# Second layer of a two-layer MLP: Strassen products over pairs of 512-token blocks instead of over the halves of one block

## The chip, the cores and the metric

One core of one Trainium2 chip. The metric is the device time of one execution in microseconds (us), the median of several runs.

## What is computed

An attention with few packed keys gives x (4608 tokens of 512 features). Two feed-forward layers follow, each 512 to 2048 to 512 features:

```python
def _moe_ref(x, w_in, w_out):
    h = x @ w_in                                   # 4608x512 @ 512x2048
    sp = np.where(h > 20.0, h, np.log1p(np.exp(np.minimum(h, 20.0))))
    g = h * np.tanh(sp)
    return (g @ w_out).astype(np.float32)          # 4608x2048 @ 2048x512

def _moe2_ref(x, w_in, w_out):
    h = x @ w_in
    g = h - np.tanh(h)
    return (g @ w_out).astype(np.float32)

attn_out = _attn_ref(**attn_kwargs)                # 8 batches, 8 heads, 576 tokens, 64 features
x = np.ascontiguousarray(attn_out.transpose(0, 2, 1, 3)).reshape(B * S, H * D)
x = _moe_ref(x=x, **moe_kwargs)
return _moe2_ref(x=x, **moe2_kwargs)
```

All of it is float32. Each matrix product is made of three passes over operands split into a high and a low part (high by high, high by low, low by high; `PASSES`), each a matmul of its own.

## The kernel before

**Blocks.** Tokens lie along the columns. There are nine blocks of 512 tokens: blocks 0 to 7 are the first 512 tokens of each batch, block 8 (the rest block) is the last 64 of all eight. The first layer (`layer1`, `layer1_rest`) leaves its output y of each block in DRAM (`y_d`).

**Second layer.** For each block, `load_y` loads y, and ScalarE (ACT) and VectorE (DVE) make from it the seven Strassen operands, split into high and low. Strassen's two by two runs over two halves of the features, two halves of w_in's 2048 columns, and two halves of the block's tokens, `HB` = 256 columns each. The seven combinations of the weights were made earlier and lie in `w2i_d`. `pair2` does one pair p of 128-wide chunks (fc = p and p + 8) of the 2048: seven products of six matmuls of 256 columns each (L856), the copies of three of them out of PSUM by ACT (L867), the additions into h by DVE (L870), and the last copy by ACT (L888). `second` then computes g of each chunk with 5 ACT and 6 DVE instructions, and adds g times w_out into four accumulators, `acc`, with 12 matmuls of 512 columns (L923). So a pair is 42 matmuls of 256 columns and 24 of 512. After eight pairs the accumulators are copied out (L929) and stored. All of w_out (16 tiles `wo` of 512 KB) is loaded once (`load_second`) and stays; each pair's weights `m` come anew for each block.

**Order.** A planner (`Plan.emit`) writes the instructions of all engines out in one order: every operation has a key (a due time), costs and buffers, and each engine takes the available operation of the lowest key. On the chip each engine follows its own list in order, waiting on semaphores. All loads and stores are issued by SyncE (SP), in its list's order, through the helper at L323. Buffers are taken from named kinds (`wo`, `a2`, `x`, `m`, `bk` for PSUM banks), some of them in the order of the keys (`queue`).

Of the kernel before, what the change touches and what calls it, by code (L numbers as in the profile page):

```python
# [49 lines left out]
class Buf:  # L50
# [21 lines left out]
class Plan:  # L72
# [44 lines left out]
    def emit(self):  # L117
# [18 lines left out]
        while left:  # L136
# [107 lines left out]
def tile_packed_attention_mish_tanhshrink(  # L244
# [43 lines left out]
    for nm, n in (("yh", 7), ("tt", 2), ("pc", 6)):  # L288
# [9 lines left out]
    w2o_d = dr.tile([16, 128, 2, 512], F32, name="w2o_d")  # L298

# [492 lines left out]
    def load_y(blk, sw):  # L792
        k0 = kb(NPAIR * blk) - 8
        f, ld = [], []
        for i in range(2):
            f.append(Buf(K["yv" if i == 0 else "yh"], [128, 2, TB]))
            ld.append(dma(lambda i=i: f[i].tile,
                          lambda i=i: y_d[2 * i:2 * i + 2, :, blk * TB:(blk + 1) * TB].rearrange("k p t -> p k t"), 512,
                          k0 - 15 + i, [y_st[blk, i], sw], [f[i]]))
# [12 lines left out]
        def split(j, kd, i, t, after, k):  # L812
# [5 lines left out]
            yq[blk, j], yq_rd[blk, j] = o, l  # L818
# [5 lines left out]
        st1 = split(2, "yh", 0, 0, [t1], k0 + 2.6)  # L824
        t3 = sub(0, 1, (1, 1), (0, 1), [t1] + ld, k0 + 3.3)
        s22 = split(4, "yh", 1, 1, ld[1:], k0 + 3.9)
        t2 = sub(1, 1, (1, 1), (0, 0), [s22, t1, t3], k0 + 4.6)
        st2 = split(3, "yh", 1, 1, [t2], k0 + 5.2)
        t4 = sub(1, 0, (1, 1), (1, 0), [t2, s21], k0 + 6.0)
        split(5, "yh", 0, 1, [t3], k0 + 6.5)  # L830
        split(6, "yh", 1, 0, [t4], k0 + 7.8)

    acc2, o_, g4_last = {}, {}, {}

    def pair2(n, sw):
# [12 lines left out]
        def product(j, slot, bk, deps, take, first):
            w = (wm[j // 4], wm_rd[j // 4])
# [13 lines left out]
        hb = [Buf(K["x"], [128, TB]) for _ in range(2)]
        c1, c5, cy = (Buf(K["pc"], [128, HB]) for _ in range(3))

        def copy(c, bk, slot, deps):
            return op("ACT", a_cost(HB, True), lambda: A.activation(c.tile, bk.tile[:, :HB], AF.Copy), ks(slot), deps, [c])  # L867

        def add(half, tok, bk, c, slot, deps, take, give):
            return op("DVE", v_cost(HB), lambda: V.tensor_tensor(  # L870
                out=hb[half].tile[:, HB * tok:HB * tok + HB], in0=bk.tile[:, :HB], in1=c.tile, op=ALU.add),
                ks(slot), deps, take, give)
# [13 lines left out]
        c22 = add(1, 1, ba, c5, 21, [p7, s5], [hb[1]], [c5])
        p4 = product(6, 30, ba, [p7, c22], [], False)
        c21 = op("ACT", a_cost(HB, True), lambda: A.activation(hb[1].tile[:, :HB], ba.tile[:, :HB], AF.Copy),  # L888
                 ks(31), [p4, c22], give=[ba])
        second(blk, p, hb[0], [c11, c12], ks(20), k0, (41, 42, 43, 44))  # L890
        second(blk, p + 8, hb[1], [c21, c22], ks(32), k0, (52, 53, 54, 55))
# [139 lines left out]
```

## Time and profile before

| | |
|---|---|
| Median of 3 runs | 1484.35 us (1483.98 to 1485.32) |
| The profiled execution | 1483.46 us, of which the span of the profile is 1481.7 us |
| Granted TensorE clock, mean | 0.999 |
| TensorE (PE) busy | 1463.3 us, 99% of the span |
| VectorE (DVE) busy | 1032.4 us, 70% |
| ScalarE (ACT) busy | 993.2 us, 67% |
| DMA moved | 298.52 MB, 201 GB/s |

An engine's busy time is the time in which it has an instruction running, so PE is without work for some 18 us of the span. The stages follow each other on the same engines: attention and first layer up to about 715 us, second layer from there.

### The profile page before, as it was taken

Reading aid. Unit: us, or ns where it says so; the run is one execution under the profiler, and the core shown is the slowest. Engines: PE = TensorE matmul, PEld = TensorE weight load, DVE = VectorE, ACT = ScalarE, POOL = GpSimd, SP = SyncE. Lnnn points to the kernel's source line nnn. Section 1 sums busy time; section 2 is a strip of 40 time slices with the busy share of each in tenths; the row PEclk is TensorE's granted clock in tenths of the full one; section 3 lists DMA queues with packets and bytes.
Section 4 is the critical chain, followed back from the end, with each engine's and each line's share of the span. In section 5 each row is a group of like instructions: output and inputs, shape, how many; then the busy total and the mean of one; then the engine's idle time right before and its main releaser. Section 6 shows DMA issues by size and latency. Waiting matters only on the chain.

```text
span 1481.7 us, 26083 instructions
## 1 busy us (share of the span) xinstructions
PE 1463.3 (99%) x10078; PEld 1273.0 (86%) x10078; DVE 1032.4 (70%) x1924; ACT 993.2 (67%) x1980; POOL 0.2 (0%) x4
## 2 busy tenths in 40 slices
PE   8999999999999999999999999999999999999998
PEld 5898888788888888888898989999999999999996
DVE  6995575746575524214589797888979797888885
ACT  5987675766666555434577667676867676776765
POOL 0000000000000000000000000000000000000000
PEclk9999999999999999999999999999999999999999
DMA  9897585857674532238655546464646565555552
GB/s 335 266 328 257 178 277 185 262 177 253 211 254 161 172 113 76 82 127 299 233 197 207 199 181 227 180 226 153 253 153 224 182 224 184 203 203 193 190 187 51
DMA packets 118380, 298.52 MB, mean 201 GB/s; under 512 B 31856, under 2 KB 41200, under 8 KB 109040
## 3 DMA queue, kind: packets, MB, share of 16 engines
q1 hardware_dynamic: 117968, 296.66, 57.9%
q8 instruction: 79, 1.29, 0.4%
q14 instruction: 45, 0.37, 0.1%
q10 hardware_dynamic: 288, 0.20, 0.0%
HBM read 246.48 MB, written 50.33 MB: 200 GB/s over the span
## 4 chain that ended last, share of the span: by engine, by line
PE 94%; DMA 3%; ACT 2%; DVE 0%; issue 0%; SPq 0%; ACTq 0%
PE acc L923 26%; PE acc L699 26%; PE bk L856 24%; PE bk L729 13%; PE bk L667 2%; PE bk L585 1%; DMA m<-w2i_d 1%; PE bk L537 1%; PE bk L611 0%; PE bk L564 0%; DMA y_d<-yv 0%; DMA st<-in_w1o 0%; DMA st<-in_w1i 0%; DMA x<-in_q 0%; DMA ident<-in_eye 0%; ACT st L343 0%
## 5 line engine op out<-in xcount | busy, mean ns | idle before, releaser
L699 PE MATMUL acc<-g,wo 128*128 128x512 f32 (+2 forms) x1920 | 430.6, 372 | 1.1 <-DVE wo L365 0.7
L923 PE MATMUL acc<-g,wo 128*128 128x512 f32 x1728 | 407.6, 390 | 1.2 <-ACT g L912 1.0
L699 PEld LDWEIGHTS acc<-g,wo 128*128 128x128 f32 x1920 | 327.9, 188 | 64.6 <-issue 11.9
L923 PEld LDWEIGHTS acc<-g,wo 128*128 128x128 f32 x1728 | 318.8, 188 | 65.4 <-ACT g L912 1.4
L856 PE MATMUL bk<-yh,m 128*128 128x256 f32 x2160 | 297.4, 283 | 1.2 <-DMA m<-w2i_d 0.5
L856 PEld LDWEIGHTS bk<-yh,m 128*128 128x128 f32 x2160 | 280.7, 191 | 9.4 <-DVE x L870 2.3
L729 PEld LDWEIGHTS bk<-a,m 128*128 128x128 f32 x1536 | 216.5, 188 | 19.4 <-issue 3.5
L729 PE MATMUL bk<-a,m 128*128 128x288 f32 x1536 | 229.2, 296 | 1.5 <-DVE m L678 0.8
L719 DVE TENSOR_TENSOR g<-e,g 128x512 fp32r<-128x512 f32 (+2 forms) x144 | 99.1, 689 | 147.6 <-ACT g L718 146.1
L733 ACT ACTIVATE e<-bk 128x288 f32<-128x288 f32 x256 | 103.6, 409 | 141.8 <-PE bk L729 140.5
L912 ACT ACTIVATE g<-xw 128x512 fp32r<-128x512 f32 x144 | 90.6, 629 | 150.2 <-DVE xw L910 145.7
L870 DVE TENSOR_TENSOR x<-bk,pc 128x256 f32<-128x256 f32 x216 | 89.7, 418 | 83.4 <-PE bk L856 83.4
L856 PE MATMUL bk<-a,m 128*128 128x256 f32 x864 | 127.2, 283 | 0.0
L913 DVE TENSOR_TENSOR g<-xw,g 128x512 fp32r<-128x512 f32 x144 | 99.2, 689 | 37.3 <-ACT g L912 37.2
L856 PEld LDWEIGHTS bk<-a,m 128*128 128x128 f32 x864 | 114.1, 192 | 0.4 <-ACT x L888 0.2
L910 DVE COPY_PREDICATED xw<-e,tt 128x512 f32<-128x512 uint32 x144 | 109.2, 759 | 1.7
L902 DVE SCALAR_TENSOR_TENSOR xw<-xw,xw 128x512 f32<-128x512 f32 x144 | 98.6, 685 | 8.0 <-ACT xw L900 7.9
L718 ACT ACTIVATE g<-e 128x512 fp32r<-128x512 f32 (+2 forms) x144 | 91.0, 632 | 19.1 <-PE acc L699 15.2
L898 ACT ACTIVATE xw<-e,c_qb 128x512 f32<-128x512 f32 x144 | 102.8, 714 | 0.0
L908 DVE TENSOR_TENSOR tt<-x,tt 128x512 f32<-128x512 f32 x144 | 98.9, 687 | 1.4 <-ACT tt L901 0.9
L897 ACT ACTIVATE e<-x 128x512 f32<-128x512 f32 x144 | 90.6, 629 | 13.6 <-DVE x L870 11.6
L906 DVE SCALAR_TENSOR_TENSOR xw<-xw,x 128x512 f32<-128x512 f32 x144 | 98.8, 686 | 0.0
(107 smaller groups left out, 1255.4 us busy)
## 6 DMA issues: line engine op xcount, KB each, us to landing
m<-w2i_d SPq DMA_DIRECT2D x72, 1024.0 KB, 5.1
m<-w2i_d SPq DMA_DIRECT2D x72, 768.0 KB, 6.2
xw<-w1i_d SPq DMA_DIRECT2D x112, 256.0 KB, 4.1
w2i_d<-x SPq DMA_DIRECT2D x56, 256.0 KB, 2.8
x<-in_q SPq DMA_DIRECT2D x64, 144.0 KB, 3.8
y_d<-yv SPq DMA_DIRECT2D x18, 512.0 KB, 4.3
out_t<-x SPq DMA_DIRECT2D x36, 256.0 KB, 2.7
st<-in_w1i SPq DMA_DIRECT2D x16, 512.0 KB, 5.2
```

Of the source, the lines that this page charges most:

```text
L699: T.matmul(ac.tile[:, c0:c1], r(wo[fc].tile[:, wl, oc * 128:(oc + 1) * 128]), r(gv(gl)), start=first and c0 == 0 and i == 0, stop=last and ...
L719: return gt, op("DVE", v_cost(n), lambda: V.tensor_tensor(out=r(gt.tile[:, 1]), in0=ev(), in1=gt.tile[:, 0], op=ALU.subtract), kf + 1.2, [ ...
L729: T.matmul(h.tile[:, :HALF], r(m.tile[:, fc % 4, kc, wl, :]), r(x.tile[:, kc, al, :]), start=(i == 0), stop=(i == 5))
L733: return op("ACT", a_cost(HALF, True), lambda: A.activation(out(), h.tile[:, :HALF], AF.Mish), k0 - 2.5, [g1] + after, take, [h], table="m ...
L856: T.matmul(bk.tile[:, :HB], r(wv[:, kc, wl, :]), r(yq[blk, j].tile[:, kc, yl, :]), start=(first and i == 0), stop=(i == 5), skip_group_che ...
L898: p1 = op("ACT", a_cost(TB, False, True), lambda: A.activation(s1.tile, zz.tile, AF.Sigmoid, bias=c_qb, scale=Q_L), k0 + 0.1, [sq], [s1])
L902: q = op("DVE", v_cost(TB), lambda: V.scalar_tensor_tensor(out=s1.tile, in0=s1.tile, scalar=Q_E, in1=s2.tile, op0=ALU.add, op1=ALU.mult), ...
L906: q = op("DVE", v_cost(TB), lambda: V.scalar_tensor_tensor(out=s1.tile, in0=s1.tile, scalar=Q_A, in1=h.tile, op0=ALU.mult, op1=ALU.mult), ...
L908: d = op("DVE", v_cost(TB), lambda: V.tensor_tensor(out=tt.tile, in0=h.tile, in1=tt.tile, op=ALU.subtract), k0 + 1.3, [th], give=[h])
L910: q = op("DVE", v_cost(TB), lambda: V.copy_predicated(s1.tile, zz.tile.bitcast(U32), tt.tile), k0 + 1.4, [q, d, k], give=[zz, tt])
L913: lo = op("DVE", v_cost(TB), lambda: V.tensor_tensor(out=r(gt.tile[:, 1, :]), in0=s1.tile, in1=gt.tile[:, 0, :], op=ALU.subtract), k0 + 2. ...
L923: T.matmul(ac.tile, r(w2c[fc].tile[:, wl, oc * 128:(oc + 1) * 128]), r(gt.tile[:, gl, :]), start=(fc == 0 and i == 0), stop=(fc == NFC - 1 ...
```

## The change

The blocks 0 to 7 are taken in pairs (super-blocks 0 to 3), and Strassen's two token halves are now the two blocks of a pair: a product has 512 columns. The rest block stays as it was, with 256. Four things go with it:

- The operands of the four super-blocks are made while the first layer runs (`combos`), written to DRAM (`yq_d`), and loaded by `load_sup`: 14 loads of 512 KB for a super-block, into four `a2` and ten `wo` buffers.
- These take the place of w_out, which is now fetched anew for each block (`fetch_out`), with at most six tiles held at a time (`cap_w`).
- `products` and the output matmuls have keys of their own (`prod_key`, `out_key`): a pair's products give h of both blocks; the first block's outputs run between the products, the second block's later, among the next super-block's first products. h of the second block waits in 13 buffers `hq`.
- A planner rule for queued buffers is loosened (`b in k.queue[:need[k]]`), and the Sigmoid and Tanh table is loaded earlier.

```diff
-                                    turn = turn and (k.queue is None or k.queue[0] is b)
+                                    turn = turn and (k.queue is None or b in k.queue[:need[k]])
...
+    yq_d = dr.tile([B // 2, 7, 2, 128, 2, TB], F32, name="yq_d")
...
+    C0, C1 = (103, 109, 115, 128.5), 14.0
+
+    def combos(s, kc):
+
+        k0 = ka(C0[s]) + C1 * kc
+        late = s == NSUP - 1
...
+        def split(j, i, t, after, k):
+            o, ov = bufs("xw", j)
+            h = op("ACT", a_cost(TB), lambda: A.activation(r(ov(0)), b(i, t), AF.Copy), k, after, o)
+            l = op("DVE", v_cost(TB), lambda: V.tensor_tensor(
+                out=r(ov(1)), in0=b(i, t), in1=ov(0), op=ALU.subtract), k + 0.5, [h], give=held((i, t)))
...
-    def load_second(sw):
-        for fc in range(NFC):
-            w2c[fc] = Buf(K["wo"], [128, 2, 512])
-            w2c_rd[fc] = dma(lambda fc=fc: w2c[fc].tile, lambda fc=fc: w2o_d[fc], 512,
-                             kb(fc % 8) + fc // 8, [w2_st[16 + fc], sw], [w2c[fc]])
...
+    PR, OU = 9.52, 5.44
+    PER = NPAIR * (PR + 2 * OU)
+
+    def base(s):
+        return ka(NA + NFC) - NPAIR * OU + s * PER
+
+    def prod_key(s, p):
+        if s == NSUP:
+            return base(s) + 23 + (PR + OU) * p
+        return base(s) + (22 + 20 * p if p < 2 else 62.6 + (PR + OU) * (p - 2))
...
+    def fetch_out(s, half, p):
+        for c in range(2):
+            fc = p + 8 * c
+            w = w2c[s, half, fc] = Buf(K["wo"], [128, 2, 512], cap=K["cap_w"])
+            w2c_rd[s, half, fc] = dma(lambda w=w: w.tile, lambda fc=fc: w2o_d[fc], 512,
+                                      out_key(s, half, p) - 12 + c, [w2_st[16 + fc]], [w])
...
+    def load_sup(s):
+        for n, j in enumerate(range(7)):
+            for kc in range(2):
+                yq[s, j, kc] = Buf(K["a2" if j < 2 else "wo"], [128, 2, TB])
+                yq_rd[s, j, kc] = dma(lambda j=j, kc=kc: yq[s, j, kc].tile, lambda j=j, kc=kc: yq_d[s, j, kc], 512,
+                                      prod_key(s, 0) - 24 + 1.5 * n, yq_st[s, j, kc], [yq[s, j, kc]])
...
-                        T.matmul(bk.tile[:, :HB], r(wv[:, kc, wl, :]), r(yq[blk, j].tile[:, kc, yl, :]),
-                                 start=(first and i == 0), stop=(i == 5),
+                        y = ys[kc].tile[:, yl, :] if full else ys[0].tile[:, kc, yl, :]
+                        T.matmul(bk.tile[:, :n], r(wv[:, kc, wl, :]), r(y), start=(first and i == 0), stop=(i == 5),
                                  skip_group_check=not first)
...
-        p1 = product(0, 2, ba, [act2[0]], [ba], True)
-        s1 = copy(c1, ba, 3, [p1])
-        p2 = product(1, 4, bb, [], [bb], True)
-        c11 = add(0, 0, bb, c1, 5, [p2, s1], [hb[0]], [bb, c1])
-        p5 = product(2, 6, bc, [], [bc], True)
-        s5 = copy(c5, bc, 7, [p5])
-        p6 = product(3, 16, ba, [p1, s1], [], False)
+        p1 = product(0, 0, ba, [sw], [ba], True)
+        s1 = copy(c1, ba, 0.5, [p1])
+        p2 = product(1, 1, bb, [], [bb], True)
+        c11 = add(0, 0, bb, c1, 1.5, [p2, s1], [bb, c1])
+        p5 = product(2, 2, bc, [], [bc], True)
+        s5 = copy(c5, bc, 2.5, [p5])
+        p6 = product(3, 3, ba, [p1, s1], [], False)
+        sy = copy(cy, ba, 3.5, [p6])
+        p3 = product(4, 4, bc, [p5, s5], [], False)
+        c12 = add(0, 1, bc, cy, 4.5, [p3, sy, c11], [bc, cy])
+        p7 = product(5, 5, ba, [p6, sy], [], False)
+        c22 = add(1, 1, ba, c5, 5.5, [p7, s5], [c5])
+        p4 = product(6, 6, ba, [p7, c22], [], False)
```

**Where the order changes: a pair's products on PE.** Before, in the middle of the second layer, the seven products (lines L856, a row of six matmuls each) of neighbouring pairs stand interleaved (m_9632 and m_9621 are the weights of two pairs), and each is followed by another bank's product:

```order
L856 MATMUL bk_9625<-yh_8819,m_9632 128x256 x6
L856 MATMUL bk_9746<-yh_9756,m_9621 128x256 x6
L856 MATMUL bk_9877<-a_2_8874,m_9741 128x256 x6
L856 MATMUL bk_9790<-yh_9694,m_9754 128x256 x6
L856 MATMUL bk_9900<-a_3_8893,m_9741 128x256 x6
L856 MATMUL bk_9746<-yh_9777,m_9754 128x256 x6
L856 MATMUL bk_9922<-yh_8979,m_9741 128x256 x6
L923 MATMUL acc_0_9107<-g_9840,wo_7934 128x512 x3
```

Now, within super-block 0, one pair's products (L942 of the changed kernel, two rows of three matmuls each; here the third to the seventh) stand in one run on three banks, two output groups (L1027) ahead of the last:

```order
L942 MATMUL bk_10422<-wo_9230,m_10175 128x512 x3
L942 MATMUL bk_10422<-wo_9235,m_10175 128x512 x3
L942 MATMUL bk_10391<-wo_9247,m_10175 128x512 x3
L942 MATMUL bk_10391<-wo_9252,m_10175 128x512 x3
L942 MATMUL bk_10422<-wo_9267,m_10220 128x512 x3
L942 MATMUL bk_10422<-wo_9273,m_10220 128x512 x3
L942 MATMUL bk_10391<-wo_9279,m_10220 128x512 x3
L942 MATMUL bk_10391<-wo_9283,m_10220 128x512 x3
L1027 MATMUL acc_0_10044<-g_10271,wo_10090 128x512 x3
L1027 MATMUL acc_0_10050<-g_10271,wo_10090 128x512 x3
L942 MATMUL bk_10391<-wo_9303,m_10220 128x512 x3
L942 MATMUL bk_10391<-wo_9306,m_10220 128x512 x3
```

The fifth product writes bank bk_10422 again, one product after the third left it, and the sixth bk_10391 one product after the fourth; the last follows the sixth on one bank with six output matmuls between.

**Where the order changes: SP's loads at the turn of a block.** Before, at the turn from one block to the next, SP's list holds the pairs' weights and two loads of y:

```order
L323 DMA m_9741<-w2i_d 128x2048
L323 DMA m_9754<-w2i_d 128x1536
L323 DMA yv_9798<-y_d 128x2x512
L323 DMA yh_9823<-y_d 128x2x512
L323 DMA m_9872<-w2i_d 128x2048
L323 DMA m_9884<-w2i_d 128x1536
```

Now, at the turn from super-block 0 to 1, the 14 operand loads stand together (the first eight, four into `a_`, four into `wo_`, are ahead of these rows), with both weights of the second pair among them, and the next tiles of w_out come behind:

```order
L324 DMA m_10780<-w2i_d 128x2048
L324 DMA wo_10791<-yq_d 128x1024
L324 DMA wo_10797<-yq_d 128x1024
L324 DMA wo_10803<-yq_d 128x1024
L324 DMA wo_10807<-yq_d 128x1024
L324 DMA wo_10827<-yq_d 128x1024
L324 DMA wo_10830<-yq_d 128x1024
L324 DMA m_10838<-w2i_d 128x1536
L324 DMA wo_10845<-w2o_d 128x1024
L324 DMA wo_10873<-w2o_d 128x1024
L324 DMA wo_10902<-w2o_d 128x1024
L324 DMA wo_10930<-w2o_d 128x1024
```

On PE, 138 matmuls of 512 columns stand from the first product of super-block 0's last pair to the first that reads wo_10845: that pair's 42, 24 and 48 of outputs, and the first 24 of super-block 1's products.

**Where the order changes: PE's end.** Before, 36 matmuls stand behind the last product:

```order
L856 MATMUL bk_16477<-yh_15684,m_16473 128x256 x6
L923 MATMUL acc_0_15963<-g_16645,wo_7934 128x512 x3
L923 MATMUL acc_0_15973<-g_16645,wo_7934 128x512 x3
L923 MATMUL acc_0_15980<-g_16645,wo_7934 128x512 x3
L923 MATMUL acc_0_15985<-g_16645,wo_7934 128x512 x3
L923 MATMUL acc_0_15963<-g_16673,wo_7948 128x512 x3
```

Now it is 69 (the rest of one chunk, of which these rows show the start, and five whole ones of 12):

```order
L942 MATMUL bk_15125<-wo_14156,m_14967 128x256 x6
L1027 MATMUL acc_0_14628<-g_15001,wo_14867 128x512 x3
L1027 MATMUL acc_0_14637<-g_15001,wo_14867 128x512 x3
L1027 MATMUL acc_0_14644<-g_15001,wo_14867 128x512 x3
L1027 MATMUL acc_0_14618<-g_15037,wo_14894 128x512 x3
L1027 MATMUL acc_0_14628<-g_15037,wo_14894 128x512 x3
```

The last product moved ahead of 33 more output matmuls.

## Rows read from the trace of the kernel before

**Rows 1.** The page, part 1: busy time, share, instructions.

```profile
PE 1463.3 (99%) x10078; PEld 1273.0 (86%) x10078; DVE 1032.4 (70%) x1924; ACT 993.2 (67%) x1980; POOL 0.2 (0%) x4
```

**Rows 2.** Windows: length, busy time by engine (PE, PEld, DVE, ACT, POOL), clock, DMA.

```profile
909.00:1246.00 337.00, 336.86 (x2109) 304.94 (x2109) 282.95 (x524) 241.17 (x492) 0.00 (x0) 1.00 0.55 200
580.00:660.00 80.00, 80.00 (x488) 68.08 (x487) 24.05 (x37) 35.34 (x69) 0.00 (x0) 1.00 0.30 97
660.00:707.00 47.00, 47.00 (x222) 39.47 (x222) 18.56 (x29) 19.29 (x32) 0.00 (x0) 1.00 0.77 271
707.00:740.00 33.00, 32.02 (x198) 28.55 (x197) 20.32 (x40) 20.20 (x42) 0.00 (x0) 1.00 0.70 246
1451.00:1482.00 31.00, 23.41 (x116) 19.07 (x114) 17.61 (x32) 14.76 (x28) 0.00 (x0) 0.94 0.16 35
```

**Rows 3.** The chain that ended last, 815 to 990 us: start, length, work.

```profile
818.76 5.49 PE acc L923 x24
...
834.75 5.03 PE bk L856 x42
839.78 5.47 PE acc L923 x24
...
903.16 5.47 PE acc L923 x24
```

**Rows 4.** Groups of instructions: the second layer's matmuls.

```profile
L923 PE MATMUL acc<-g,wo 128*128 128x512 f32 x1728 | 407.6, 390 | 1.2 <-ACT g L912 1.0 <-DVE g L913 0.2
...
L856 PE MATMUL bk<-yh,m 128*128 128x256 f32 x2160 | 297.4, 283 | 1.2 <-DMA m<-w2i_d 0.5 <-DVE x L870 0.4
...
L856 PE MATMUL bk<-a,m 128*128 128x256 f32 x864 | 127.2, 283 | 0.0
```

**Rows 5.** Groups: reads of PSUM by ACT and DVE, of 256 and 512 columns.

```profile
L870 DVE TENSOR_TENSOR x<-bk,pc 128x256 f32<-128x256 f32 x216 | 89.7, 418 | 83.4 <-PE bk L856 83.4
...
L867 ACT ACTIVATE pc<-bk 128x256 f32<-128x256 f32 x216 | 79.3, 370 | 5.6 <-PE bk L856 5.6
...
L678 DVE TENSOR_TENSOR m<-bk,m 128x512 fp32r<-128x512 f32 x64 | 42.1, 676 | 6.6 <-ACT m L676 6.6
...
L929 ACT ACTIVATE x<-acc 128x512 f32<-128x512 f32 x36 | 19.7, 605 | 1.8 <-PE acc L923 1.6
```

**Rows 6.** Waits of PE's weight loads, 740 to 1414 us: total, times, longest.

```profile
PEld bk L856 <- DVE x L870: 1.6, 7, 0.2
```

**Rows 7.** Timeline of ACT, 840 to 862 us: start, length, instruction, idle before.

```profile
846.00 0.38 ACT L888 ACTIVATE x<-bk 128x256 f32<-128x256 f32 x1 [0.20 <-PE bk L856]
...
850.17 0.72 ACT L898 ACTIVATE xw<-e,c_qb 128x512 f32<-128x512 f32 x1
850.79 0.62 ACT L900 ACTIVATE xw<-e 128x512 f32<-128x512 f32 x1
```

**Rows 8.** Groups: one of y's operand instructions on DVE.

```profile
L815 DVE TENSOR_TENSOR yh<-yh,yh 128x512 fp32r<-128x512 f32 x27 | 18.5, 686 | 2.1 <-ACT yh L814 2.1
```

**Rows 9.** DMA issues: count, size, median us to landing.

```profile
m<-w2i_d SPq DMA_DIRECT2D x72, 1024.0 KB, 5.1
m<-w2i_d SPq DMA_DIRECT2D x72, 768.0 KB, 6.2
...
wo<-w2o_d SPq DMA_DIRECT2D x16, 512.0 KB, 4.4
```

**Rows 10.** Windows of 5 us with much DMA; columns as in rows 2.

```profile
680.00:685.00 5.00, 5.00 (x24) 4.14 (x23) 1.39 (x2) 1.26 (x2) 0.00 (x0) 1.00 0.98 343
685.00:690.00 5.00, 5.00 (x24) 4.14 (x23) 2.96 (x5) 2.77 (x5) 0.00 (x0) 1.00 1.05 419
```

**Rows 11.** Timeline of the end, 1464 to 1475 us.

```profile
1464.79 0.88 PE L856 MATMUL bk<-yh,m 128*128 128x256 f32 x6
...
1472.15 0.49 PE L923 MATMUL acc<-g,wo 128*128 128x512 f32 x1 [1.01 <-ACT g L912]
...
1472.87 2.79 PE L923 MATMUL acc<-g,wo 128*128 128x512 f32 x11 [0.23 <-DVE g L913]
```

More of the change, by code (lines that the diff above doesn't have):

```diff
@@ L845, in pair2, with product @@
             wm_rd.append(dma(lambda i=i: wm[i].tile, lambda j0=j0, j1=j1: w2i_d[p, :, j0:j1], 256 * (j1 - j0),
-                             k0 - 26 + 11 * i, [w2_st[p, j] for j in range(j0, j1)] + [sw], [wm[i]]))
-        def product(j, slot, bk, deps, take, first):
-            w = (wm[j // 4], wm_rd[j // 4])
+                             k0 - 20 + 5 * i, [w2_st[p, j] for j in range(j0, j1)], [wm[i]]))
+        def product(j, i, bk, deps, take, first):
+            ys = [yq[s, j, kc] for kc in range(2 if full else 1)]
             def f():
@@ L862, in pair2 @@
         ba, bb, bc = (bank(K["cap_2"]) for _ in range(3))
[L863 to L872, printed above, removed]
@@ L886, in pair2, with hv @@
[L886 to L891, printed above, removed]
-    def second(blk, fc, h, rd, k0, k1, slots):
-        zz, tt, s1 = Buf(K["e"], [128, TB]), Buf(K["tt"], [128, TB]), Buf(K["xw"], [128, TB])
-        s2 = Buf(K["xw"], [128, TB])
+        if full:
+            hb = [[Buf(K["x"], [128, TB]), Buf(K["hq" if p < 6 else "x"], [128, TB])] for _ in range(2)]
+            def hv(half, tok):
+                return hb[half][tok].tile
+        else:
+            hb = [[Buf(K["x"], [128, TB])] * 2 for _ in range(2)]
+            def hv(half, tok):
+                return hb[half][0].tile[:, HB * tok:HB * tok + HB]
@@ new lines, in products, with copy, add @@
+        c1, c5, cy = (Buf(K["pc"], [128, TB]) for _ in range(3))
+        def copy(c, bk, i, deps):
+            return op("ACT", a_cost(n, True), lambda: A.activation(c.tile[:, :n], bk.tile[:, :n], AF.Copy), ks(i) - 12, deps,
+                      [c])
+        def add(half, tok, bk, c, i, deps, give):
+            take = [hb[half][tok]] if full or half == tok else []
+            return op("DVE", v_cost(n), lambda: V.tensor_tensor(
+                out=hv(half, tok), in0=bk.tile[:, :n], in1=c.tile[:, :n], op=ALU.add), ks(i) - 12, deps, take, give)
@@ new lines, in products @@
+        c22 = add(1, 1, ba, c5, 5.5, [p7, s5], [c5])
+        p4 = product(6, 6, ba, [p7, c22], [], False)
+        c21 = op("ACT", a_cost(n, True), lambda: A.activation(hv(1, 0), ba.tile[:, :n], AF.Copy),
+                 ks(6.5) - 12, [p4, c22], [hb[1][0]] if full else [], give=[ba])
+        ev = ((c11, c12), (c21, c22))
+        for half in range(2):
+            fc = p + 8 * half
+            if not full:
+                second(s, 0, fc, hb[half][0], list(ev[half]), ks(7 + 2 * half), out_key(s, 0, p) + OU / 2 * half)
+                continue
+            second(s, 0, fc, hb[half][0], [ev[half][0]], ks(4 + 3 * half), out_key(s, 0, p) + OU / 2 * half)
+            second(s, 1, fc, hb[half][1], [ev[half][1]], ks(25 + 5 * half), out_key(s, 1, p) + OU / 2 * half)
@@ L896, in second @@
+    def second(s, half, fc, h, rd, k0, ko):
+        zz, tt, s1, s2 = (Buf(K[k], [128, TB]) for k in ("e", "tt", "xw", "xw"))
         gt = Buf(K["g"], [128, 2, TB])
+        first, last = fc == 0, fc == NFC - 1
         sq = op("ACT", a_cost(TB), lambda: A.activation(zz.tile, h.tile, AF.Square), k0, rd, [zz])
         p1 = op("ACT", a_cost(TB, False, True), lambda: A.activation(
-            s1.tile, zz.tile, AF.Sigmoid, bias=c_qb, scale=Q_L), k0 + 0.1, [sq], [s1])
-        p2 = op("ACT", a_cost(TB), lambda: A.activation(s2.tile, zz.tile, AF.Tanh, scale=Q_T), k0 + 0.15, [sq], [s2])
@@ L913, in second @@
         lo = op("DVE", v_cost(TB), lambda: V.tensor_tensor(
[L914 removed]
+            out=r(gt.tile[:, 1, :]), in0=h.tile, in1=gt.tile[:, 0, :], op=ALU.subtract), max(k0 + 2.1, ko - 5.9), [a],
+            give=[h])
+        w = w2c[s, half, fc]
         for oc in range(4):
[L916 to L919 removed]
+            if first:
+                acc2[s, half, oc] = Buf(K["acc", oc], [128, 512])
+            ac = acc2[s, half, oc]
@@ L921, in f @@
             def f(oc=oc, ac=ac):
                 for i, (wl, gl) in enumerate(PASSES):
-                    T.matmul(ac.tile, r(w2c[fc].tile[:, wl, oc * 128:(oc + 1) * 128]), r(gt.tile[:, gl, :]),
-                             start=(fc == 0 and i == 0), stop=(fc == NFC - 1 and i == 2))
-            g4_last[oc] = z = op("PE", 0.69, f, ko, [lo, w2c_rd[fc], g4_last.get(oc)],
-                                 [ac] if fc == 0 else [], [gt])
-            if fc == NFC - 1:
+                    T.matmul(ac.tile, r(w.tile[:, wl, oc * 128:(oc + 1) * 128]), r(gt.tile[:, gl, :]),
+                             start=(first and i == 0), stop=(last and i == 2))
```

166 lines of the change are left out of this document (112 added, 54 removed).

## The prediction, made before the changed kernel was run

> **What bounds it now.** I read the page's busy times first: PE is busy 99% of the span, DVE 70%, ACT 67% [rows 1]. The windows by stage say where the rest is: in the middle of the second layer PE is busy 336.86 of 337 us, in the late first layer all of 80 and of 47; only the stretch between the layers (0.98 us idle of 33) and the end (7.6 of 31) leave PE without work [rows 2]. So the time is the sum of PE's matmuls, and other engines, queues and transfers count only where they make PE wait. The chain shows the beat of the second layer: 42 matmuls of 256 columns in 5.03 us, then 24 of 512 in 5.47 us, over and over [rows 3]. That is 119.8 ns for a matmul of 256 columns and 227.9 ns for one of 512: half the columns cost 53% of the time, so each matmul carries a fixed part of about 11.7 ns (2 x 119.8 - 227.9). The means in the groups (283 and 390 ns) are lengths of overlapping records and no price [rows 4].
>
> **The change, part by part.** The sum is made against the profiled execution, 1483.46 us (span 1481.7 and 1.8 around it), which lies 0.9 us under the median of 1484.35; the difference is then put on the median.
>
> *Products.* Of 3024 matmuls of 256 columns [rows 4] the order of the changed kernel keeps 336 (the rest block's 8 pairs of 42). 2688 go, 1344 of 512 columns come. For one pair of chunks and two blocks: 2 x 5.03 = 10.06 us before; 42 x 0.2279 = 9.57 now; 0.49 us less, 32 times: **-15.6 us**. The output matmuls stay as they are. No row has a product of 512 columns; the nearest row is the output matmul, which has the same shapes, a weight load for each matmul, and accumulates in PSUM, so I take its price. The bounds are that price and two narrow ones (no gain).
>
> *Block turns.* Eight pairs take 8 x 10.50 = 84.0 us, but from one block's turn to the next it is 903.16 - 818.76 = 84.40 [rows 3]. In the second layer PE's weight loads wait 7 times, 0.2 us each, for the DVE addition L870 [rows 6], about once a block. At the turn y's operands are made on DVE (11 instructions of 0.69 us for a block [rows 8]), and the addition stands behind one. The change moves this work into the first layer, so I take the eight turns' 0.40 as gone: **-3.2 us** (bounds 0 and -3.2).
>
> *End.* Before, behind the last product, which ends at about 1465.7, PE runs 24 matmuls and then stands 1.01 and 0.23 us for the last g [rows 11]. The g that waited longest was there 7.2 us after that product (1472.87). Now 69 matmuls, 15.7 us, stand behind the last product, so g is there in time: **-1.2 us** (bounds 0 and -1.2).
>
> *Copies out of PSUM.* New in the order is a tight place: a bank is written again one product, 1.37 us, after it was left, twice behind an ACT copy, once behind a DVE addition. ACT begins 0.20 us after PE's end [rows 7] and takes 0.61 for 512 columns [rows 5]: 0.81, so 0.56 is left, and an instruction under way holds ACT for at most 0.62 (850.17 to 850.79 [rows 7]): late by 0.06 at worst. DVE takes 0.68 [rows 5], 0.88 with the start, 0.49 left; an instruction of 0.69 [rows 8] under way makes it late by 0.20 at worst, which is what the longest wait of before was [rows 6]. At worst 32 x (0.06 + 0.06 + 0.20) = 10 us; the worst needs an instruction that has just begun each time, so I take 0.05 a pair: **+1.5 us** (bounds 0 and 10). What hides the copies is the next product alone; without that cover it would be 0.8 us for each.
>
> *Load of the engines.* DVE was busy 282.95 of 337 us, 84% [rows 2]. It loses y's 11 x 0.69 = 7.6 us of each 84.4 (9%), and for two blocks three additions of 0.68 take the place of six of 0.418 [rows 5], 2% more: some 73%. ACT loses as well. Neither becomes the bound.
>
> *Turns of super-blocks.* w_out is now streamed, and the 14 operand loads can start only as the last pair frees their buffers; behind them in SP's list stand the next tiles of w_out, for which PE waits. From the end of that pair's first product to the first matmul that reads such a tile PE has the 138 matmuls counted in the order less that product: 138 x 0.2279 - 1.37 = 30.1 us. In that time 14 x 512 + 1024 + 768 + 512 KB = 9.70 MB must pass. At the 343 to 419 GB/s of busy windows [rows 10] this is 28.3 to 23.1 us; the last tile then needs what a lone load takes beyond its bytes, 4.4 [rows 9] - 1.3 = 3.1 us. So it lands between 3.9 us early and 1.3 late. I take **+0.5 us** for the three such turns (bounds 0 and 4). Elsewhere in a super-block the volume is far from the limit: some 41 MB in 164 us, 250 GB/s, where it was 200 [rows 2]. The Trainium skill (DMA: Bandwidth & Descriptors, section Bandwidth) speaks against this: it puts the HBM limit of one core at about 358 GB/s. By it the 9.70 MB take 27.1 us and the tile lands 0.1 late, which leaves the sum where it is; the window of 419 GB/s shows that for 5 us more can pass.
>
> *From first to second layer.* Here the most is added: between the first operand load and the last store of super-block 3's operands, SP's list now holds 14 operand loads, 28 stores of 256 KB, 8 loads of y, the rest block's loads, six weights and first tiles of w_out, about 30.6 MB in some 95 us of PE's matmuls: 322 GB/s, where 271 and 246 were moved [rows 2]. Stores that wait for ACT and DVE stand ahead of operand loads in the one queue, and six products of the first pair each wait for such a load. Queueing made the 768 KB load land later than the 1024 KB one, 6.2 to 5.1 us [rows 9]; if each of the six is late by that 1.1 us, it is 6.6 us. Most have output matmuls of the rest block ahead of them, so I take a third: **+2 us** (bounds 0 and 6.6).
>
> *First layer.* The other six half-combinations add 42 ACT copies (26 us at 0.61), 66 DVE instructions (45 us at 0.69), and 28 MB within some 140 us. ACT was busy 35.34 of 80 us there, DVE 24.05, DMA moved 97 GB/s, PE was never idle [rows 2]: all of it has room. What could cost is an ACT or DVE instruction that waits for its load with Mish evacuations behind it: **+0.5 us** (bounds 0 and 3).
>
> Sum: -15.6 - 3.2 - 1.2 + 1.5 + 0.5 + 2 + 0.5 = **-15.5 us**: 1468.0 for such a profiled execution, 1468.9, so **1469** us, for the median.
>
> **Rivals.** *Transfers eat half of it.* If the turns get only 320 GB/s, a tile lands 30.3 + 3.1 - 30.1 = 3.3 us late, three times 10 us, or the transition takes its 6.6 and the copies half their bound: 1475 to 1481. For it: 9.70 MB follow each other without a pause, and a window at 0.98 of the engines' time moved only 343 GB/s. Against it: 419 in the next. At 302 GB/s the gain would be gone.
>
> *The DVE addition becomes the bound: slower.* If one more DVE instruction than the one under way stands ahead of the addition before the last product, the product waits 0.20 + 0.68 + 2 x 0.69 - 1.37 = 0.89 us in each of 32 pairs, 28.5 us in the place of the 1.5: about 1496. It decides from about 0.5 us a pair on. For it: before, neighbouring pairs were interleaved and gave every bank more cover. Against it: DVE has a quarter of its time free, and its list has a single instruction between this addition and the one before it.
>
> *The wide product costs two narrow ones.* Then the -15.6 is missing: about 1484. For it: no product of that width is in the trace. Against it: 1728 output matmuls of that width run at 227.9 ns in the same stream [rows 3, 4]. The Trainium skill (TensorE: Matmul & The Clock Gate, section Back-to-back issue gap) gives a matmul N/2.4 + 2.5 ns, 109 and 216 ns; by that the saving is 1344 x 2.5 ns = 3.4 us and the time about 1481. The rows show a fixed part more than four times as large, and they decide.
>
> *All costs are nothing:* -20.0 us, about 1464.
>
> **Chances.** Forecast (1465 to 1475) 0.64; costs nothing or a dearer fixed part (under 1465) 0.08; transfers (1475 to 1481) 0.18; wide product no cheaper 0.04; slower by the addition 0.06. The range 1462 to 1478 holds the first two and half of the third, 0.8. A measurement tells some 0.2% (3 us) from no change: faster 0.90, same 0.04, slower 0.06.
>
> **What would show it.** The chain of the changed kernel in mid super-block: 24 wide products in 5.47 us, six more at 1.37 each, no idle time on PE in that stretch beyond tenths of a us a pair; waits of PE for ACT copies and DVE additions under 3 us in all; no wait for w_out tiles or operands of over 1 us at the three turns; no wait over 0.3 us behind the last product; between the layers PE idle of about 3 us. The prediction is wrong if a product of six takes 1.44 us, if PE waits for the DVE addition in each pair by more than 0.3 us, or if the DMA windows at the turns stay under 320 GB/s.

## The result and the profile after

The changed kernel takes **1462.99 us** (median of six runs, 1460.96 to 1469.62); the kernel before takes 1485.39 beside it (six runs, 1483.98 to 1490.25). The ratio is 0.9854, 95% interval 0.9829 to 0.9879: faster by 22.4 us, 1.5%, where 15.5 us were forecast. The profiled execution takes 1462.25 us with a span of 1460.1, against 1483.46 and 1481.7: 21.6 us of span to account for.

The page's busy times, as in [rows 1]:

```profile
PE 1444.2 (99%) x8734; PEld 1201.1 (82%) x8734; DVE 1026.1 (70%) x1828; ACT 981.8 (67%) x1852; POOL 0.2 (0%) x4
```

PE still bounds the kernel: 19.1 us of the 21.6 are busy time of PE, the other 2.5 its idle time (18.4 before, 15.9 now).

The windows by stage, with the columns of [rows 2]: the late first layer, the stretch between the layers, the second layer, the end.

```profile
660.00:707.00 47.00, 46.57 (x211) 38.49 (x210) 20.16 (x31) 21.51 (x36) 0.00 (x0) 1.00 0.93 343
707.00:740.00 33.00, 33.00 (x148) 27.31 (x147) 22.51 (x38) 20.77 (x38) 0.00 (x0) 1.00 0.94 345
740.00:1414.00 674.00, 674.00 (x3071) 558.75 (x3070) 534.07 (x921) 460.35 (x847) 0.00 (x0) 1.00 0.70 248
1420.00:1461.00 41.00, 34.14 (x189) 29.30 (x188) 20.92 (x38) 18.56 (x35) 0.00 (x0) 0.97 0.28 87
```

In 674 us of the second layer PE has no idle time in the records (they overlap, so waits of some tenths show in the chain below and not here). Between the layers the DMA engines are at 0.93 and 0.94, and PE idles 0.43 us in those 80 us, where it was 0.98 [rows 2]. All of it is one wait, the only one of PE that is listed from 640 us on (total, times, longest):

```profile
PE acc L700 <- ACT yv L709: 0.4, 1, 0.4
```

The chain that ended last, in mid super-block and from one turn of super-blocks to the next (start, length, work), as in [rows 3]:

```profile
896.95 8.16 PE bk L942 x36
905.11 1.36 PE acc L1027 x6
906.47 1.39 PE bk L942 x6
...
983.19 14.96 PE acc L1027 x66
998.15 5.44 PE bk L942 x24
...
1136.02 8.31 PE bk L942 x36
...
1147.05 14.96 PE acc L1027 x66
1162.01 5.44 PE bk L942 x24
...
1310.79 31.28 PE acc L1027 x138
```

Here the change can be read to a hundredth. A product of six wide matmuls takes 1.36 us, seven take 9.52; 24 wide ones, products or outputs, take 5.44, so 226.7 ns each. A super-block, two blocks, takes 1162.01 - 998.15 = 163.86 us, and from the next of the long output runs to the last (1147.05 to 1310.79) 163.74; twice a block of before is 168.80 [rows 3]. That is 5 us less. With no wait at all a super-block would be 8 x 9.52 + 16 x 5.44 = 163.20, so some 0.6 of it is waiting: a run of 36 matmuls of 8.31 instead of 8.16 is what such a wait looks like here.

The waits of PE's weight loads, 740 to 1430 us (total, times, longest), as in [rows 6]:

```profile
PEld bk L942 <- ACT pc L962: 3.3, 13, 0.3
PEld bk L942 <- DVE x L967: 1.0, 4, 0.3
PEld acc L1027 <- ACT x L1034: 0.7, 3, 0.2
```

The copies out of PSUM are late 13 times in 32 pairs, by 0.3 us at most. At 1125 us, for one, ACT has begun another instruction (1125.03) as the product ends (1124.97); the copy runs from 1125.55 to 1126.14, and the weight load that waits for its bank starts at 1126.18, 0.28 us late. Weight loads run ahead of their matmuls, so only 0.15 of it reaches the chain.

The turn of super-blocks: three windows of 5 us (columns as above), then SP's timeline where the first w_out loads behind the operands are issued, then the issues in 970 to 1010 us with the median time to landing.

```profile
985.00:990.00 5.00, 5.00 (x24) 4.14 (x23) 4.51 (x9) 5.00 (x11) 0.00 (x0) 1.00 1.02 418
...
1000.00:1005.00 5.00, 5.00 (x23) 4.13 (x22) 5.00 (x10) 4.97 (x11) 0.00 (x0) 1.00 1.03 408
1005.00:1010.00 5.00, 5.00 (x23) 4.13 (x22) 4.90 (x9) 2.27 (x4) 0.00 (x0) 1.00 1.06 425
```

```profile
991.06 5.54 SPq L324 DMA_DIRECT2D wo<-w2o_d  x5
```

```profile
wo<-w2o_d SPq DMA_DIRECT2D x9, 512.0 KB, 10.7
```

With the median of 10.7 us the first of these tiles lands at about 1001.8, an estimate; the outputs that need it start at 1003.59 (the end of the 24 products above). It is some 1.8 us early.

The end, in PE's timeline:

```profile
1438.31 15.83 PE L1027 MATMUL acc<-g,wo 128*128 128x512 f32 x69
```

The 69 matmuls behind the last product run without a wait; the 1.01 and 0.23 of [rows 11] are gone.

### The profile page after: what moved, and what is told of

It is laid out like the page before. It is cut to its first block, busy times and chain, and to the rows that moved or that the text cites. A ratio compares the mean times of both kernels' runs of the same rounds, so it can differ in the third digit from the quotient of the medians.

```text
span 1460.1 us, 23589 instructions
## 1 busy us (share of the span) xinstructions
PE 1444.2 (99%) x8734; PEld 1201.1 (82%) x8734; DVE 1026.1 (70%) x1828; ACT 981.8 (67%) x1852; POOL 0.2 (0%) x4
## 4 chain that ended last, share of the span: by engine, by line
PE 95%; DMA 2%; ACT 2%; DVE 1%; issue 0%; ACTq 0%; SPq 0%
PE acc L1027 27%; PE acc L700 26%; PE bk L942 24%; PE bk L730 13%; PE bk L668 2%; DMA y_d<-yv 1%; PE bk L586 1%; PE bk L612 1%; PE bk L538 1%; PE bk L565 1%; DMA st<-in_w1o 0%; DMA st<-in_w1i 0%; ACT st L344 0%; DMA ident<-in_eye 0%; ACT yv L709 0%
## 5 line engine op out<-in xcount | busy, mean ns | idle before, releaser
L1027 PE MATMUL acc<-g,wo 128*128 128x512 f32 x1728 | 410.2, 390 | 0.0
L1027 PEld LDWEIGHTS acc<-g,wo 128*128 128x128 f32 x1728 | 322.4, 188 | 66.2 <-ACT x L1034 0.7
L942 PE MATMUL bk<-wo,m 128*128 128x512 f32 (+1 forms) x1200 | 265.8, 370 | 0.0
L942 PEld LDWEIGHTS bk<-wo,m 128*128 128x128 f32 x1200 | 210.2, 188 | 43.1 <-ACT pc L962 3.3
L730 PEld LDWEIGHTS bk<-a,m 128*128 128x128 f32 x1536 | 216.4, 188 | 19.6 <-issue 3.5
L942 PE MATMUL bk<-a,m 128*128 128x512 f32 (+1 forms) x480 | 106.1, 368 | 0.0
L942 PEld LDWEIGHTS bk<-a,m 128*128 128x128 f32 x480 | 84.8, 188 | 15.7
L1009 DVE TENSOR_TENSOR tt<-x,tt 128x512 f32<-128x512 f32 x96 | 66.7, 694 | 42.4 <-ACT tt L1004 42.4
L1002 ACT ACTIVATE xw<-e 128x512 f32<-128x512 f32 x144 | 89.3, 620 | 0.2 <-DVE x L1011 0.2
L1015 ACT ACTIVATE g<-x 128x512 fp32r<-128x512 f32 x96 | 59.4, 626 | 39.1 <-PE acc L1027 32.8
L962 ACT ACTIVATE pc<-bk 128x512 f32<-128x512 f32 (+1 forms) x120 | 65.5, 546 | 29.0 <-PE bk L942 28.7
L1016 DVE TENSOR_TENSOR g<-x,g 128x512 fp32r<-128x512 f32 x96 | 66.2, 693 | 14.7 <-ACT g L1015 14.7
L1013 DVE COPY_PREDICATED x<-e,tt 128x512 f32<-128x512 uint32 x96 | 73.4, 764 | 0.8
```

What stands on the lines that cost most here:

```text
L730: T.matmul(h.tile[:, :HALF], r(m.tile[:, fc % 4, kc, wl, :]), r(x.tile[:, kc, al, :]), start=(i == 0), stop=(i == 5))
L942: T.matmul(bk.tile[:, :n], r(wv[:, kc, wl, :]), r(y), start=(first and i == 0), stop=(i == 5), skip_group_check=not first)
L1002: p2 = op("ACT", a_cost(TB), lambda: A.activation(s2.tile, zz.tile, AF.Tanh, scale=Q_T), k0 + 0.15, [sq, act2[0]], [s2])
L1009: d = op("DVE", v_cost(TB), lambda: V.tensor_tensor(out=tt.tile, in0=h.tile, in1=tt.tile, op=ALU.subtract), k0 + 1.2, [th])
L1013: q = op("DVE", 0.645, lambda: V.copy_predicated(h.tile, zz.tile.bitcast(U32), tt.tile), k0 + 1.4, [q, d, k], give=[zz, tt])
L1027: T.matmul(ac.tile, r(w.tile[:, wl, oc * 128:(oc + 1) * 128]), r(gt.tile[:, gl, :]), start=(first and i == 0), stop=(last and i == 2))
```

## The experiments

The kernel before was run beside each on the same chip; its median was 1484.84 us beside e1, e2, e4 and e5, 1483.8 beside e6, e7, e8 and e11, and 1485.33 beside e9, e10, e12 and e13.

**e1_split: the width alone.** Everything as in the changed kernel, but a wide product is two runs of six matmuls of 256 columns.

```diff
-                for kc in range(2):
-                    for wl, yl in PASSES:
-                        y = ys[kc].tile[:, yl, :] if full else ...
-                        T.matmul(bk.tile[:, :n], ...
+                for c0 in range(0, n, HB):
+                    for kc in range(2):
+                        for wl, yl in PASSES:
+                            y = ys[kc].tile[:, yl, c0:c0 + HB] if full else ...
+                            T.matmul(bk.tile[:, c0:c0 + HB], ...
```

> The changed kernel with each product of 512 columns issued as two runs of six matmuls of 256 columns, into the two halves of the same bank; the order of everything else stays. Theory (the gain is the fixed part of each matmul): a pair's products go from 9.52 us back to 10.06 and 24 output matmuls from 5.44 back to 5.47, so 32 x 0.54 + 64 x 0.03 = 19.2 us are lost, and the time is about 1481 us, ratio to before 0.997 to 0.999. Rival (the gain is the moving of y's operands and the better turns; the width is worth a few us only): about 1466 us, ratio 0.988.

Measured: 1481.99 us (ten runs), ratio 0.9986 (0.9973 to 0.9999). Its chain in mid super-block:

```profile
924.61 8.63 PE bk L943 x72
933.24 1.39 PE acc L1029 x6
934.63 1.43 PE bk L943 x12
936.06 4.11 PE acc L1029 x18
```

8.63 + 1.43 = 10.06 us for the 84 narrow matmuls, exactly two times the 5.03 of [rows 3]: 119.8 ns each. So some 19 of the 22.4 us gained are the width (1481.99 - 1462.99). The output matmuls, 24 in 1.39 + 4.11 = 5.50, cost more again than the 5.44 they take beside wide products, though nothing about them was edited.

**e2_before_no_y, e9_before_y_bufs, e10_before_no_y_y_bufs: the block turns alone.** e2 is the kernel before without the making of y's operands: seven loads of w_out's tiles stand in for them. e9 is the kernel before with the copies of the last two blocks' first-layer accumulators going to four buffers of their own (the edit is shown with e7). e10 has both.

```diff
     def load_y(blk, sw):
-        f, ld = [], []
...
+        for j in range(7):
+            o = Buf(K["a2" if j < 2 else "yh"], [128, 2, 2, HB])
...
+                                lambda j=j: w2o_d[j].rearrange("p l n -> p (l n)"), 512,
```

> The kernel before without the making of y's operands in the second layer: the 7 ACT copies and 11 DVE instructions of each block are left out, and w_out's tiles are loaded in the operands' place (7 loads of 512 KB a block for 2), so its products are not those of y. Theory (the 0.40 us of each block turn come from the addition L870 behind those DVE instructions): the block period falls from 84.40 to 84.0 us, PE's weight loads no longer wait for L870, 3 us in all: ratio 0.998. Rival (the turn's loss is the order of PE at the turn): the period stays 84.4, ratio 1.000. Rival that this move is the gain: ratio 0.99 or less.

> The kernel before with the four buffers for the copies of blocks 7 and 8 (as in the changed kernel's variant). It is the base for the next run. No PE wait for the copy at about 676 us; median within 2 us of before, ratio 0.999 to 1.000.

> The same, without the making of y's operands in the second layer (7 ACT copies and 11 DVE instructions of each block left out, w_out's tiles loaded in their place, so the products are not those of y). Theory (the turns' 0.40 us a block come from that work, and in the earlier run without it a wait of 2.3 us at the layers' seam and the half clock behind it took them back): the block period is 84.0 us, and the time is 3 us under that of the kernel with the buffers alone, ratio to before 0.997 to 0.998. Rival (the turns' loss was not on the path): the period is 84.0 and the time the same, 0.999 to 1.000.

Measured: e2 1485.8 us, ratio 1.0006 (0.9997 to 1.0016): no gain in the time. Yet e10 takes 1480.58, ratio 0.9971 (0.9959 to 0.9983), and e9 1484.24, ratio 0.9994 (0.9985 to 1.0003): with the four buffers the same step is worth 3.7 us. The chain of e10 over two blocks:

```profile
817.46 5.47 PE acc L902 x24
...
901.46 5.47 PE acc L902 x24
...
985.46 4.56 PE acc L902 x20
```

84.00 us twice, where [rows 3] gave 84.40: the turn's 0.40 goes with the operands. What e2 lost instead stands in its timeline of PE near the end of the first layer, and in the window behind it (clock 0.93):

```profile
678.14 24.13 PE L699 MATMUL acc<-g,wo 128*128 128x512 f32 x98 [2.34 <-ACT yv L708]
```

```profile
680.00:700.00 20.00, 20.00 (x83) 16.39 (x83) 5.74 (x9) 5.64 (x9) 0.00 (x0) 0.93 0.87 304
```

PE waits 2.34 us for an ACT copy whose buffer is still being stored, and PE's clock is granted at 0.93 of 2.4 GHz in the 20 us behind (a part of them at 1.2), which costs 20 x 0.07 = 1.4 us more. The profile of before has no such wait. So the profiled execution of e2 carried a second difference of about the same size; e9 and e10 were made to take it out.

**e4_copy2, e5_add2: how tight the copies are.** Each copy of a wide product out of PSUM (e4), or each addition into h (e5), is issued twice, with the same operands and the same output.

```diff
-    lambda: A.activation(c.tile[:, :n], bk.tile[:, :n], AF.Copy)
+    lambda: [A.activation(c.tile[:, :n], bk.tile[:, :n], AF.Copy) for _ in range(2 if full else 1)]
```

> The changed kernel with each copy of a 512-column product out of PSUM issued twice on ACT (3 a pair), the planned order unchanged. It leaves the cover of 1.36 us with 0.20 + 0.48 + 0.61 = 1.29 us of work, 0.07 us to spare instead of 0.55. If the copies are near to being the bound, any ACT instruction under way (ACT is busy two thirds of the time, 0.52 to 0.62 us each) then makes PE wait, 0.2 us on average for each of two copies: 32 x 0.4 = 13 us, about 1475 us. If they have more room than I reckon: under 3 us, 1465.

> The changed kernel with each of the three DVE additions of a 512-column product issued twice, the planned order unchanged: 0.20 + 0.60 + 0.68 = 1.48 us behind a cover of 1.36, so the last product of each pair waits at least 0.12 us and, with an instruction under way or the doubled addition ahead, 0.7: 32 x 0.12 to 0.7 = 4 to 22 us, 1466 to 1484. If the addition has slack elsewhere: no change, 1462.

Measured: 1501.17 and 1515.22 us, one run each: 38 and 52 us above the changed kernel. Both are above what was expected. The waits of PE in e4, and in e5 (740 to 1430 us):

```profile
PE bk L942 <- ACT pc L962: 21.4, 28, 1.3
```

```profile
PE bk L942 <- DVE hq L967: 21.9, 20, 2.0
PE bk L942 <- DVE x L967: 9.1, 8, 1.1
PE bk L942 <- ACT pc L962: 4.1, 10, 0.4
```

Only the doubled instruction's own engine is waited for in e4. From one turn of super-blocks to the next e4's chain takes 172.3 us (848.03 to 1020.36) and e5's 177.3 (846.81 to 1024.11), where the changed kernel takes 163.8: 1.1 and 1.7 us more a pair. A pair has three copies of some 0.6 us, so 1.8 us more work on ACT, and 1.1 of it reaches PE; of the additions' three times 0.7 it is 1.7. So little slack is left there: the changed kernel's pair is within one instruction of being set by ACT or DVE at these places, although in the changed kernel ACT is free a third of the second layer and DVE a fifth (460.35 and 534.07 busy of 674 us). In e5 one stretch of 20 us in each of three super-blocks is also at a lower clock (960 to 980 us: PE busy 18.12 of 20, clock 0.91), some 1.8 us each, 0.2 a pair; in e4 the clock is 1.00 in these super-blocks.

**e6_no_combos: what the operands' making costs in the first layer.** The half-combinations, their stores and their waits are left out; the operand loads read tiles of w_out.

```diff
-    for sup in range(NSUP):
-        for kc in range(2):
-            combos(sup, kc)
```

> The changed kernel without the making and storing of the super-blocks' operands in the first layer (56 ACT copies, 88 DVE instructions, 38 MB left out; w_out's tiles are loaded in the operands' place, so the products are not those of y). Theory (that work is hidden under PE's matmuls): PE's idle time up to 740 us stays within 1.5 us of the 9.9 of the changed kernel, time 1459 to 1463 us. Rival (it costs waits in the first layer or in the transition): 1455 us or less.

Measured: 1460.72 us, one run, 0.24 under the lowest of the changed kernel's six. Up to 740 us PE idles 9.0 us, where the changed kernel has 9.9: what the making costs there is some 0.9 us, the rest of it is hidden.

**e11_turn_more: how full the turn is.** Four copies of 512 KB from DRAM to DRAM are issued among the last operand loads of each of the three turns.

```diff
+                    if s and j > 4:
+                        SP.dma_start(dump_d[s, 2 * (j - 5) + kc], w2o_d[2 * j + kc])
```

> The changed kernel with four copies of 512 KB from DRAM to DRAM in each of the three turns between super-blocks, issued among the last operand loads, ahead of w_out's next tiles; the planned order of the rest unchanged. Theory (the turn is full: the first tile lands 1.8 us ahead of its use, at 410 GB/s): 2.1 MB more take at least 5 us, so PE waits 3 us or more at each turn, 10 to 25 us in all with the half clock that a wait may bring, 1472 to 1487 us. Rival (the turn has room): under 2 us in all, 1464 us.

Measured: 1477.52 us, one run, 14.5 above the changed kernel. The waits of PE from 640 us on, and the window behind one of the turns:

```profile
PE acc L1031 <- DMA wo<-w2o_d: 8.4, 3, 3.7
PE acc L701 <- ACT yv L710: 2.2, 1, 2.2
```

```profile
1000.00:1020.00 20.00, 16.29 (x66) 12.93 (x65) 15.01 (x27) 12.51 (x24) 0.00 (x0) 0.91 1.01 410
```

2.1 MB at 410 GB/s are 5.1 us; less the 1.8 us that the tile is early, 3.3 a turn are due, and 2.8 are seen. The other wait, for the copy at the end of the first layer, stands in e12 too, without the edit. The remaining 4 of the 14.5 us were not taken apart; behind the waits the clock is granted at a lower level for a part of the time (0.91 above). The turn is hidden by some 2 us and no more.

**e7_y_bufs, e8_y_bufs_order: what is left.** e7 gives the copies of the last two blocks' first-layer accumulators four buffers with stores of their own, so that none waits for a store. e8 also issues p5 and its copy ahead of p2 and its addition, which takes the addition off the way of the copy.

```diff
+            if blk >= B - 1:
+                yo = Buf(K["x"], [128, TB])
...
+                s = dma(lambda oc=oc: y_d[oc, :, blk * TB:(blk + 1) * TB], lambda yo=yo: yo.tile, 256, k0 + TA, [ev],
+                        give=[yo])
...
+                continue
             if oc % 2 == 0:
                 yv, done = Buf(K["yv"], [128, 2, TB]), []
...
-        p2 = product(1, 1, bb, [], [bb], True)
-        c11 = add(0, 0, bb, c1, 1.5, [p2, s1], [bb, c1])
-        p5 = product(2, 2, bc, [], [bc], True)
-        s5 = copy(c5, bc, 2.5, [p5])
+        p5 = product(2, 1, bc, [], [bc], True)
+        s5 = copy(c5, bc, 1.5, [p5])
+        p2 = product(1, 2, bb, [], [bb], True)
+        c11 = add(0, 0, bb, c1, 2.5, [p2, s1], [bb, c1])
```

> The changed kernel with the copies of the first layer's accumulators of blocks 7 and 8 going to four buffers of 256 KB each, with stores of their own, in the place of one buffer of 512 KB that waits for its store. Theory (the runs of one kernel differ by up to 8 us because at about 676 us PE waits up to 2.4 us for that copy, which waits for the store of the buffer before, and then runs some us at half clock): no wait there, no clock below 1.00 between 660 and 740 us, the median falls by 0.4 to 3 us to 1460 to 1462, and the spread of the runs falls to about 3 us. Rival (the spread comes from elsewhere): the wait goes, median and spread stay (1463, 8 us).

> The same, and in each pair the third product (p5) is issued ahead of the second (p2), so that the copy of its bank has two products, 2.7 us, ahead of the bank's next use instead of one. Theory (in the changed kernel PE's weight loads wait 3.3 us for ACT's copies in 13 of 32 pairs, half of them for this copy): these waits fall to about half, the time by 1 to 1.5 us against the kernel with the buffers alone, which a ratio can hardly show; the profile's waits do. Rival (ACT's list is in the way, and the wait moves to the other copies or to the addition): the waits stay at 4 to 5 us in all.

Measured: e7 1463.68 us (1462.08 to 1465.67), ratio 0.9868 (0.9852 to 0.9883); e8 1462.78 (1461.13 to 1463.92), ratio 0.9863 (0.9847 to 0.988). Neither differs from the changed kernel by more than the intervals. In e7's profile the wait for the copy at the layers' seam is gone, but the gain expected of it does not show in the median. In e8's profile the waits for the copies out of PSUM are all but gone (those for the additions are 1.7 us, where they were 1.0), a super-block takes 163.5 us where e7's takes 163.8, and one wait for an operand has come:

```profile
PEld bk L953 <- ACT pc L973: 0.2, 1, 0.2
```

```profile
PE bk L953 <- DMA wo<-yq_d: 1.2, 1, 1.2
```

**e12_changed_again, e13_y_bufs_order_again: the changed kernel and e8 on one chip.** Both as they were.

> The changed kernel, as it is, beside the next one on the same chip. 1461 to 1465 us.

> The changed kernel with the four buffers and p5 ahead of p2. If both waits that it takes away are on the path, it is 1.5 to 3 us under the changed kernel on the same chip; if they are hidden or come back elsewhere, the two agree within 1 us.

Measured: the changed kernel 1466.4 us (1464.79 to 1467.59), ratio 0.9869 (0.9855 to 0.9884); e13 1461.43 (1460.67 to 1461.76), ratio 0.9836 (0.9822 to 0.9849). The four runs of e13 lie under the four of the changed kernel, by 5.0 us in the median: of the versions that leave no work out it has the lowest median, though e8, the same kernel on another chip, took 1462.78. The chains of e12 and of e13, from the last long output run of the first layer to the second layer's turns:

```profile
665.15 6.82 PE acc L700 x30
...
680.24 6.42 PE acc L700 x27
686.66 2.72 PE bk L942 x12
...
1003.48 5.44 PE bk L942 x24
...
1167.29 2.72 PE bk L942 x12
```

```profile
662.86 19.04 PE acc L700 x84
681.91 2.72 PE bk L953 x12
...
998.26 5.44 PE bk L953 x24
...
1161.69 3.40 PE bk L953 x15
```

e12 enters this stretch 2.3 us later; it takes 21.51 us for what e13 does in 19.05 (the wait for the store, 2.5 us); from there to the first turn shown 0.5 more, over two super-blocks; and the next super-block takes 163.81 for 163.43 us: 0.4, the order of the copies. So between these two profiled executions, 5.7 us of span apart, two known edits give 2.5 and some 1.2 us; the 2.3 us from ahead of 665 us are a difference that no edit explains.

## Why the prediction was right, and where its sizes were off

The measured 1463 us lies inside the range that was given, but only 1 us from its lower end, and outside the 1465 to 1475 that had most of the chances: it is the case that had 0.08, that costs are nothing or the fixed part is dearer. Both came in part. The mechanism held (PE bounds the kernel, and the fixed part of its matmuls is most of the gain); the sum was 6 us too small.

The span's 21.6 us, from the rows above: products 32 x (10.06 - 9.52) = 17.3; outputs 64 x 0.03 = 1.9; block turns 7 x 0.40 = 2.8; waits for copies 4 x 0.6 = 2.4 back; the end 1.3; between the layers 0.5. Sum 21.4; 0.2 is not placed, and the rest block is taken as unchanged.

**Products: mechanism right, 3.6 us too small.** I forecast -15.6 at 227.9 ns and got -17.3 at 226.7. The price was taken from the right row, but that row held something else: 24 outputs in 5.47 us stood between narrow products, and beside wide ones the same 24 take 5.44. I also took the outputs as unchanged; they give 1.9. The planner's own costs in the change, `PR, OU = 9.52, 5.44`, are these prices to the last digit, and I did not use them. e1 shows both together: narrow products bring back 10.06 for a pair's two blocks, and 5.50 for the outputs, and with them 1482. The fixed part of a matmul, taken as in the prediction, is thus 2 x 119.8 - 226.7 = 12.9 ns, not 11.7. The Trainium skill (TensorE: Matmul & The Clock Gate, section Back-to-back issue gap) has 2.5 ns in its formula for a single matmul's gap; the rival built on that, 1481, is refuted by the time and by the 9.52 us of a pair's products where 10.06 were.

**Block turns: mechanism right, one turn too many.** -3.2 forecast for eight turns. [rows 6] show seven waits, and the chain of before shows why: the last turn, to the rest block, takes 84.02 us and loses nothing.

```profile
1325.12 5.47 PE acc L923 x24
...
1409.14 5.47 PE acc L923 x24
```

So it is -2.8. The changed kernel's profile shows no waits at turns beyond the copies', and e10 against e9 gives 3.7 us in the time.

**End: right.** -1.2 forecast. Idle time of PE from 1420 to the span's end is 40.1 - 34.14 = 5.96 us, against 30.7 - 23.41 = 7.29 from 1451 to the span's end before [rows 2]: 1.3.

**Copies out of PSUM: right place, dearer than forecast, and the other engine.** +1.5 forecast, 2.4 measured. The prediction had an ACT copy late by 0.06 us at worst and put most of the charge on the DVE addition; the weight loads wait 3.3 us for ACT, up to 0.3 a time, and 1.0 for DVE, together more than the 3 us that it gave as the limit. What it left out is that the weight load, which waits for the bank, comes ahead of its matmul, so the cover is shorter than the 1.37 us of a product: in the case at 1125 us the load was due 0.93 us after the product's end (1126.18 - 0.28 - 1124.97). What I had as remote, that the addition becomes the bound, did not come. But e4 and e5 show it to be near: of one more instruction a copy or an addition, more than half reaches PE.

**Turns of super-blocks: right, at the good end.** 3.9 early to 1.3 late was the bound; 1.8 early is what the rows show, at 408 to 425 GB/s. +0.5 forecast, 0 measured. e11 shows that the margin is real and small.

**Between the layers: wrong in size, 2.5 us.** +2 forecast, -0.5 measured. I let the six products of the first pair each be late by a share of the queueing that [rows 9] show. The loads had 343 and 345 GB/s in those 80 us, where I had worked out 322 to be needed, and no wait for an operand stands in the waits of PE. What there is instead is a wait that I did not name: the ACT copy of the last first-layer accumulators stands behind a store. It holds PE 0.4 us in the profile of the changed kernel and 2.2 in e12, the same kernel, so that this term came out below nothing is in part luck of the profiled execution.

**First layer: right.** +0.5 forecast; e6 shows 0.9 us of idle time.

The forecast fell short by 6 us: the products' and outputs' price (3.6) and the charge between the layers (2.5) make it up, and the smaller ones nearly cancel (the copies cost 0.9 more than forecast, the block turns gave 0.4 less, the turns of super-blocks and the first layer cost 0.5 less each).

Still open: the spread of either kernel, 1483.98 to 1490.25 and 1460.96 to 1469.62. The wait for the store explains up to 2.5 us of it where a profile shows that wait (e12; e7 has none); the chain of e12 also runs 3.5 us later than the first profile's already at 665 us, and nothing that was run tells why.

## What to carry to other kernels

Where PE has no idle time, the price of a change is the price of its matmuls, and half the columns cost more than half: read it from the chain (24 in 5.44 us), not from the mean of overlapping records (390 ns), and look at what stands around the row that is taken as a price. When a sure gain does not show in the time, as in e2, look in the profile for a wait elsewhere that came with the edit or with that execution: there it was a copy whose buffer was still being stored. When products on one bank are brought closer together, ask how much longer the copy between them may get; here it was less than one instruction (e4, e5).

## What the runs showed of the chip

- DMA: 408 to 425 GB/s for 30 us without a pause (980 to 1010 us, nearly all of it loads of 512 to 1024 KB from DRAM into SBUF). The Trainium skill (DMA: Bandwidth & Descriptors, section Bandwidth) puts the HBM limit of a core at about 358 GB/s, though its table also has 425 GB/s for one core's load of 16 MB; the windows here agree with the table.
- A run of 24 wide matmuls cost 0.03 us more with narrow ones on both sides (5.47 against 5.44), and 0.06 where narrow ones also split it in two (5.50, e1).
- A wait of PE of 2 us can cost more than itself: with or behind the waits of 2.34 us (e2), 2.4 (e1, at the same place), 3.7 at most (e11) and 2.0 at most (e5) the granted clock of the 20 us there is 0.91 to 0.93, so a part of them ran at 1.2 GHz in the place of 2.4; behind that of 2.2 us in e12 (680 to 700 us) it stayed at 1.00.
